# A fourth buffer for the mixed rows, and the norm of two chunks on a pitch of 18 slots

## The chip, the cores and the metric

The kernel runs on one NeuronCore of a Trainium2 chip. The metric is the device time of one execution in microseconds (us); the median of several runs is given. The engines are called TensorE (PE in the profile), VectorE (DVE), ScalarE (ACT), GpSimd (POOL) and SyncE (SP, which only issues DMAs here). SBUF is the on-chip working memory, PSUM the memory into which TensorE accumulates.

## The reference

Attention with a sigmoid in the softmax's place, a two-dimensional Fourier mix of the result, a normalisation and a two-layer network. The batch is 8, with 12 heads, 448 positions, head dimension 64, so d_model is 768; the network's hidden width is 3072.

```python
scores = q @ k.transpose(0, 1, 3, 2) / sqrt(64) - log(448)
x = (sigmoid(scores) @ v)            # then heads side by side: 8 x 448 x 768
u = x + real(fft(fft(x, axis=1), axis=2))
un = (u - mean(u)) / sqrt(var(u) + 1e-6)      # over the last axis
out = u + relu(un @ w_ch1) @ w_ch2
```

## The kernel before

The kernel has three stages. In the **attention stage** a loop runs over 192 slots, two at a time; a slot is a quarter of the positions for one pair of heads, and 24 slots make a batch. For a pair of slots the code issues, in this order: what was put off from the pair before (`sp_next`: writes of u; `act_next`: copies on ScalarE; `dve_next`: sums and adds on VectorE), the score matmuls (L132) and sigmoids (L136), the value matmuls of the pair before (L152) with an eviction on VectorE every four slots (`xT`, L161), some units of the Fourier mix, and the extras.

Each engine takes its instructions strictly in the order in which the code issues them: `pin` chains every instruction to the one before on its engine. So the place of a step in the loop is its place in the queue.

The **mix** of a batch is a list of 36 units (`mix_units`): 24 of `stage_d` (L194), 4 of `stage_s` (L205), 8 of `add_x` (L226). It is taken from while the next batch's attention runs; `mix_some` hands out units by an estimated cost until the budget of 1.14 us for a pair of slots is used up. All units use PSUM tiles of one pool with three buffers (`ps_m`). A unit's evacuation isn't issued with it but put on `act_next` or `dve_next`, so it stands at the start of the next pair. An `add_x` unit transposes three blocks of x into a PSUM tile; VectorE then adds the mix and writes one half of a tile u (L233). A batch has four tiles u, of two halves each; they come from a tag with three buffers. When a tile is full, one or two writes to `u_dram` are put on `sp_next` (L241).

The **extras** hang on slots by `at(t, fn)`. They are, in the order in which they are registered: GpSimd's and VectorE's folds of xT (L175, L178, L181), loads of q, k and v (L106, L107, L113), the casts on GpSimd (L117) and the rests on VectorE (`ql`, `kl`, L122), the scales and the preparation of the weights from slot 170 on (`TP`), and the norm. After the extras of a slot comes the search for the largest weight (`wmax`, L264) and its loads (L259), with three buffers and two tiles of lead.

The **norm** here is that of the first two chunks of 512 rows, needed by the next stage. It goes by halves of 256 rows. `norm_plan` gives the steps of one half chunk with an offset in slots each: 0 the load of 256 rows of u (L332, one buffer); 4 and 5 the statistics of the two blocks of 128 rows (L296, L299); 6 to 10 the reciprocal root, first step three small instructions (L305 to L310), then four steps of four (L315 to L319); 11 and 13 the scaling of a block (L323) and a copy to half precision on ScalarE (L345); 12 and 14 the split on VectorE (L349) and two transposing DMAs on SyncE's queue (L351). The starts before:

```python
for c in range(2):
    for g in range(2):
        for n, fn in norm_plan(c, g, fx):
            at(24 * (4 + 2 * c + g) + LNT + n, fn)      # LNT = 2
```

The four half chunks start at slots 98, 122, 146 and 170. The preparation of one weight tile (`prep_w`) is a chain: load, ScalarE takes the absolute value (L382), VectorE clamps and shifts (L384, L386), merges twice (L390, L392), ScalarE scales (L400), SyncE stores (L401), VectorE takes the rest (L403). Three tiles are made in the last slots; their ScalarE copies stand between the sigmoids.

In the **second stage** (from about 457 us) the first chunk goes through the network while the remaining 45 weight tiles are prepared, two for each of the 24 steps. The **third stage** computes the last five chunks in a fast form. The change touches neither.

Of the kernel before, what the change touches and what calls it, by code (L numbers as in the profile page):

```python
# [9 lines left out]
F32 = mybir.dt.float32  # L10
# [13 lines left out]
DM = 768  # L24
# [12 lines left out]
LNT = 2  # L37
# [21 lines left out]
def spectral_attention_ffn(tc, q, k, v, w1, w2, cd, cs, ident_in, out):  # L59
# [8 lines left out]
    with ExitStack() as top:  # L68
# [19 lines left out]
        if True:  # L88
            c1 = mix.enter_context(tc.tile_pool(name="c1", bufs=1, side="right"))
            fx = mix.enter_context(tc.tile_pool(name="fx", bufs=1, side="right"))  # L90
# [93 lines left out]
            def mix_units(b):  # L184
                xT, xp = xts[b]
                A = fx.tile([HM, 2, 2, 386], F32, tag="A", name="A")
                ps_d, sd, ut = {}, {}, {}

                def stage_d(kp, c, par, p):
                    m = HM - kp  # L190
                    if par == 0 and p == 0:
                        ps_d[c, kp] = ps_m.tile([128, 512], F32, tag="m", name="psd")
                    ps = ps_d[c, kp]
                    nc.tensor.matmul(  # L194
                        ps[:HM, par * 193:par * 193 + 193], xp[:, kp ^ c, c, par, p],
                        cd_sb[:, c, par, p], start=(p == 0), stop=(p == 2))
                    if par == 1 and p == 2:
                        act_next.append(lambda: nc.scalar.activation(
                            A[:, kp, c].rearrange("s (i r) -> s r i", r=2),
                            ps[:HM, 0:386].rearrange("s (r i) -> s r i", r=2), AF.Copy))  # L200

                def stage_s(kp, c):
                    m = HM - kp
                    ps = ps_m.tile([128, 512], F32, tag="m", name="pss")
                    nc.tensor.matmul(  # L205
                        ps[:m, :385], cs_sb[:, kp, c, :m], A[:, kp, c, :385], start=True, stop=True)
                    if c == 1:
                        sd["Q", kp] = Q = fx.tile([128, 385], F32, tag="Q", name="Q", bufs=2)
                        act_next.append(lambda: nc.scalar.activation(Q[:m], ps[:m, :385], AF.Copy))
                    else:  # L210
                        Q = sd["Q", kp]
                        sd[kp] = [fx.tile([128, 385], F32, tag=n, name=n, bufs=2) for n in ("sm", "df")]
                        for o, op in zip(sd[kp], (ALU.add, ALU.subtract)):
                            dve_next.append(lambda o=o, op=op: nc.vector.tensor_tensor(
                                out=o[:m], in0=ps[:m, :385], in1=Q[:m], op=op))

                def add_x(kp, r, hf):

                    lo, hi = (1, HM - 1) if r and not kp else (0, HM - kp)
                    s, d = sd[kp]  # L220
                    if hf == 0:
                        ut[kp, r] = fx.tile([128, DM], F32, tag="u", name="u", bufs=3)
                    u = ut[kp, r]
                    ps = ps_m.tile([128, 512], F32, tag="m", name="psx")
                    for i in range(3):
                        nc.tensor.transpose(  # L226
                            ps[:HM - kp, i * 128:(i + 1) * 128], xT[:, hf * 3 + i, r, kp:HS:2], ident)
                    y = d if hf == r else s
                    m = HM - kp
                    ysl = y[:m, 384:0:-1] if hf else y[:m, 0:384]  # L230

                    def add():
                        nc.vector.tensor_tensor(  # L233
                            out=u[:m, hf * 384:hf * 384 + 384], in0=ps[:m, :384], in1=ysl, op=ALU.add)
                        if hf:
                            base = b * S + (0, 113, 225, 336)[2 * r + kp] - lo

                            cut = lo + (hi - lo) // 16 * 16
                            for i, j in ((lo, cut), (cut, hi)):
                                if i < j:  # L240
                                    sp_next.append(lambda i=i, j=j: nc.sync.dma_start(  # L241
                                        u_dram[base + i:base + j, :], u[i:j, :]))
                    dve_next.append(add)


                res = [(0.33, lambda kp=kp, c=c, par=par, p=p: stage_d(kp, c, par, p))
                       for kp in range(2) for c in (1, 0) for par in range(2) for p in range(3)]
                res += [(0.65, lambda kp=kp, c=c: stage_s(kp, c)) for kp in range(2) for c in (1, 0)]
                res += [(0.31, lambda kp=kp, r=r, hf=hf: add_x(kp, r, hf))
                        for kp in range(2) for r in range(2) for hf in range(2)]  # L250
                return res
# [101 lines left out]
            def norm_plan(c, g, pool):  # L353

                res = [(0, lambda: norm(c, 2 * g, 0, pool))]
                for j in range(2):
                    i = 2 * g + j
                    res += [(LEAD + j, lambda i=i: norm(c, i, 1, pool)),
                            (7 + LEAD + 2 * j, lambda i=i: norm(c, i, 7, pool)),
                            (8 + LEAD + 2 * j, lambda i=i: norm(c, i, 8, pool))]  # L360
                res += [(LEAD + n, lambda n=n: norm(c, 2 * g, n, pool)) for n in range(2, 7)]
                return sorted(res, key=lambda x: x[0])
# [101 lines left out]
            def at(t, fn):  # L464
                extra.setdefault(t, []).append(fn)
# [25 lines left out]
            for c in range(2):  # L491
                for g in range(2):
                    for n, fn in norm_plan(c, g, fx):
                        at(24 * (4 + 2 * c + g) + LNT + n, fn)


            for t in range(0, TQ + LAG + 4, 2):
# [22 lines left out]
        with ExitStack() as fast, ExitStack() as st, ExitStack() as early:  # L520
# [72 lines left out]
            while units or act_next or dve_next or sp_next:  # L593
# [4 lines left out]
                n = step % MIX_STEP  # L598
# [360 lines left out]
```

## Time and profile before

| | us |
|---|---|
| median of 3 runs | 1811.45 |
| the runs | 1807.61, 1811.45, 1819.85 |
| the profiled execution | 1808.63 |
| its span, first to last instruction | 1806.8 |

| engine | busy us | share of the span |
|---|---|---|
| PE | 1670.1 | 92% |
| DVE | 1297.8 | 72% |
| ACT | 603.1 | 33% |
| POOL | 193.6 | 11% |

The shares are means over stages with different limits. Times in the profile are us from the span's start. "x3" behind an instruction counts how many like it were merged, and the text in square brackets is the engine's idle time just before the instruction with the one that ended it. PEclk is the clock that TensorE was granted, as a share of full speed (2.4 GHz; the other level is 1.2).

### The profile page before, as it was taken

What the parts mean: (1) busy time and instruction counts of PE and PEld (TensorE: products, weight loads), DVE (VectorE), ACT (ScalarE), POOL (GpSimd) and SP (SyncE); (2) the same over time, 40 slices, a digit from 0 to 9 for tenths busy, and PEclk for the clock granted to TensorE, in tenths of its full rate; (3) what the DMA queues carried; (4) which work ended last, traced back from release to release, by engine and by line L of the source; (5) the groups of instructions that cost most, each with busy time, mean ns of one, the idle gap of its engine ahead of it and who ended that gap; (6) DMA issues with size and microseconds to landing.
All of it is one profiled execution on the core that took longest, in us unless ns stands there. A gap on an engine that the chain in (4) does not pass through costs nothing. (4 is left out here: it accounts for less than half of the span.)

```text
span 1806.8 us, 27683 instructions
## 1 busy us (share of the span) xinstructions
PE 1670.1 (92%) x10996; PEld 1069.6 (59%) x10996; DVE 1297.8 (72%) x2481; ACT 603.1 (33%) x767; POOL 193.6 (11%) x220
## 2 busy tenths in 40 slices
PE   8999999987777778999879999999999999999997
PEld 4555545543533334555447777677777767776774
DVE  4445576656777776567656888788868887887667
ACT  5444444434333332133224332333133323232221
POOL 4534344334000000000000000000000000000000
PEclk9999999998999999999989999999999999999999
DMA  7666676654666665588887563756476546556551
GB/s 243 214 207 220 222 229 219 207 167 117 217 211 211 211 212 195 182 280 309 294 303 266 227 245 145 280 202 231 152 284 224 217 178 254 216 205 249 215 223 62
DMA packets 109139, 394.95 MB, mean 219 GB/s; under 512 B 23521, under 2 KB 49362, under 8 KB 93522
## 3 DMA queue, kind: packets, MB, share of 16 engines
q1 hardware_dynamic: 109010, 393.19, 61.5%
q8 instruction: 86, 1.41, 0.3%
q14 instruction: 43, 0.35, 0.1%
HBM read 316.08 MB, written 73.92 MB: 216 GB/s over the span
## 5 line engine op out<-in xcount | busy, mean ns | idle before, releaser
L771 PE MATMUL psf<-ut,ws 128*128 128x256 f16 x3780 | 425.4, 274 | 21.4 <-DMA ws<-w_dram 11.7
L822 PE MATMUL pso<-ws,H 128*128 128x384 f16 x2520 | 423.9, 326 | 4.5 <-DVE X L777 1.8
L771 PEld LDWEIGHTS <-ws 128*128 128x128 f16 x3780 | 370.8, 98 | 74.2 <-DMA ws<-w_dram 14.8
L822 PEld LDWEIGHTS <-H 128*128 128x128 f16 x2520 | 246.3, 98 | 160.8 <-issue 5.4
L136 ACT ACTIVATE a<-sc 112x900 f32<-112x900 f32 x192 | 166.8, 918 | 157.0 <-PE sc L132 156.9
L831 DVE TENSOR_TENSOR acc<-pso,acc 128x384 f32<-128x384 f32 x350 | 183.6, 550 | 18.8 <-PE pso L822 18.8
L796 ACT ACTIVATE F<-F 128x1024 f32<-128x1024 f32 x60 | 63.5, 1058 | 357.1 <-DVE F L777 357.1
L557 PE MATMUL po<-w2h,hh 128*128 128x512 f16 (+1 forms) x384 | 131.8, 343 | 52.0 <-ACT hh L545 51.3
L152 PE MATMUL av<-a,vr 112*64 112x450 f32 x768 | 171.1, 568 | 3.8 <-DVE xT L161 3.8
L777 DVE TENSOR_TENSOR H<-F,H 128x1024 f16<-128x1024 f32 x120 | 129.5, 1087 | 48.1 <-ACT H L806 48.1
L538 PE MATMUL psh<-ut,w1h 128*128 128x512 f16 x504 | 151.2, 382 | 3.0 <-DVE hl L546 3.0
L557 PEld LDWEIGHTS <-hh 128*128 128x128 f16 x768 | 76.6, 102 | 108.6 <-ACT hh L545 61.1
L777 DVE TENSOR_TENSOR F<-X,psf 128x256 f32<-128x256 f32 x240 | 96.8, 419 | 51.8 <-PE psf L771 48.0
L557 PE MATMUL po<-w2h,hl 128*128 128x512 f16 (+1 forms) x384 | 130.8, 341 | 1.9
L806 ACT ACTIVATE H<-F 128x1792 f16<-128x1792 f32 x60 | 101.8, 1697 | 88.7 <-DVE F L777 88.7
L557 PE MATMUL po<-w2l,hh 128*128 128x512 f16 (+1 forms) x384 | 131.2, 342 | 0.0
L161 DVE TENSOR_SCALAR xT<-av 128x450 f32<-128x450 f32 x48 | 30.1, 626 | 136.2 <-PE av L152 136.2
L777 DVE TENSOR_TENSOR F<-F 128x256 f32<-128x256 f32 x240 | 91.2, 422 | 24.5 <-ACT F L796 20.5
L132 PE MATMUL sc<-qh,kh 64*112 64x450 f32 x384 | 82.2, 424 | 18.0 <-ACT a L136 13.4
L546 DVE SCALAR_TENSOR_TENSOR hl<-psh,hh 128x512 f16<-128x512 f32 x48 | 33.1, 690 | 90.5 <-ACT hh L545 90.5
L152 PEld LDWEIGHTS av<-a,vr 112*64 112x64 f32 x768 | 47.7, 139 | 82.7 <-issue 67.8
L538 PE MATMUL psh<-ut,w1l 128*128 128x512 f16 x252 | 96.1, 382 | 0.0
(89 smaller groups left out, 1954.9 us busy)
## 6 DMA issues: line engine op xcount, KB each, us to landing
ws<-w_dram SPq DMA_DIRECT2D x120, 1344.0 KB, 8.8
wr<-w_in SPq DMA_DIRECT2D x96, 768.0 KB, 4.9
t_dram<-wt SPq DMA_DIRECT2D x48, 384.0 KB, 2.3
cb<-t_dram SPq DMA_DIRECT2D x24, 768.0 KB, 5.3
qr<-q_in SPq DMA_DIRECT2D x48, 225.0 KB, 3.7
kr<-k_in SPq DMA_DIRECT2D x48, 224.0 KB, 3.4
vr<-v_in SPq DMA_DIRECT2D x24, 448.0 KB
w_dram<-ch SPq DMA_DIRECT2D x24, 384.0 KB, 5.8
```

Of the source, the lines that this page charges most:

```text
L132: nc.tensor.matmul(ps[:CP, j, :SQ], split[g, 1, kn][h, c * CP:(c + 1) * CP], split[g, 0, qn][h], start=(n == 0), stop=(n == 2))
L136: nc.scalar.activation(a, ps[:CP, :, :SQ], AF.Sigmoid, bias=-math.log(S), scale=1.0 / math.sqrt(D))
L152: nc.tensor.matmul(ps[j * D:(j + 1) * D, :SQ], vr[:, c, h * D:(h + 1) * D], a[:, j], start=(c == 0), stop=(c == 3))
L538: nc.tensor.matmul(hs[c, f], l[f][:, m], r[:, m], start=(m == n == 0), stop=(m == NCC - 1 and n == 2))
L546: nc.vector.scalar_tensor_tensor(out=hl, in0=ps, scalar=0.0, in1=hh, op0=ALU.max, op1=ALU.subtract)
L557: nc.tensor.matmul(po[n][:, at:at + hi - lo], l[:, cols], r[f][:, lo:hi], start=(f == 0 and m == 0 and at == 0), stop=(f == NFC - 1 and m ...
L771: nc.tensor.matmul(ps[:, :TH], w[:, x, a, m * 128:(m + 1) * 128], ut[y][:, b, m], start=(m == n == 0), stop=(m == n == 2))
L777: nc.vector.tensor_tensor(out=o, in0=x, in1=y, op=op)
L796: nc.scalar.activation(F[:, 0:4], F[:, 0:4], AF.Relu)
L806: nc.scalar.activation(hts[P][:, 0], F[:, 1:8], AF.Copy)
L822: nc.tensor.matmul(ps[:, :384], H[:, x, a, tp * 128:(tp + 1) * 128], w[:, y, b], start=(j == n == 0), stop=(j == 1 and n == 2))
L831: later(0, lambda: nc.vector.tensor_tensor(out=to, in0=ps[:, :384], in1=to, op=ALU.add))
```

## The change

The tag of the u tiles gets a fourth buffer. The half chunks of the norm start every 18 slots from 98 on: at 98, 116, 134 and 152. The steps and their offsets stay as they are.

```diff
@@ -219,7 +219,7 @@
                     s, d = sd[kp]
                     if hf == 0:
-                        ut[kp, r] = fx.tile([128, DM], F32, tag="u", name="u", bufs=3)
+                        ut[kp, r] = fx.tile([128, DM], F32, tag="u", name="u", bufs=4)
                     u = ut[kp, r]
@@ -491,7 +491,7 @@
             for c in range(2):
                 for g in range(2):
                     for n, fn in norm_plan(c, g, fx):
-                        at(24 * (4 + 2 * c + g) + LNT + n, fn)
+                        at(96 + 18 * (2 * c + g) + LNT + n, fn)
```

## Rows read from the trace of the kernel before

**Rows 1.** Windows: start:end, length, busy us (instructions) per engine, PEclk, DMA share, GB/s
```profile
225.00:270.00 45.00, 41.66 (x247) 22.45 (x245) 32.54 (x57) 20.48 (x27) 20.27 (x23) 0.98 0.73 224
...
540.00:585.00 45.00, 35.44 (x168) 16.84 (x168) 34.16 (x45) 15.80 (x21) 0.00 (x0) 0.92 0.62 210
```
**Rows 2.** Timeline, TensorE, transposes of x: start, us, engine, line, tile, [idle before]
```profile
266.41 0.59 PE L226 MATMUL psx<-ident,xT 128*112 128x128 f32 x3 [2.74 <-DVE u L233]
...
322.44 0.88 PE L226 MATMUL psx<-ident,xT 128*112 128x128 f32 x3 [2.10 <-DVE u L233]
...
370.73 1.25 PE L226 MATMUL psx<-ident,xT 128*113 128x128 f32 x9
...
378.10 0.59 PE L226 MATMUL psx<-ident,xT 128*112 128x128 f32 x3 [1.88 <-DVE u L233]
```
**Rows 3.** Windows of the score matmuls (L132) alone: busy us (instructions) PE, PEld
```profile
0.00:262.42 262.42, 94.36 (x732) 60.80 (x732) 0.99 0.68 220
```
**Rows 4.** Timeline, VectorE, from 262 to 267 us
```profile
262.54 0.63 DVE L161 TENSOR_SCALAR xT<-av 128x450 f32<-128x450 f32 x1 [2.25 <-PE av L152]
...
265.81 1.00 DVE L233 TENSOR_TENSOR u<-psx,df 113x384 f32<-113x384 f32 x2
```
**Rows 5.** Timeline, TensorE, score matmuls after 385 us that had to wait
```profile
411.75 0.72 PE L132 MATMUL sc<-qh,kh 64*112 64x450 f32 x2 [3.40 <-ACT a L136]
...
426.52 0.46 PE L132 MATMUL sc<-qh,kh 64*112 64x450 f32 x2 [2.92 <-ACT a L136]
...
441.97 0.71 PE L132 MATMUL sc<-qh,kh 64*112 64x450 f32 x2 [6.48 <-ACT a L136]
```
**Rows 6.** Timeline, ScalarE, three copies
```profile
367.11 0.49 ACT L209 ACTIVATE Q<-pss 112x385 f32<-112x385 f32 x1 [1.31 <-PE pss L205]
...
409.86 0.94 ACT L400 ACTIVATE w1p<-wt,wsc 128x768 f16<-128x768 f32 x1 [7.68 <-DVE wt L392]
...
424.36 0.82 ACT L345 ACTIVATE hl<-un 128x768 f16<-128x768 f32 x1
```
**Rows 7.** Timeline, VectorE, steps of the norm
```profile
278.73 1.01 DVE L296 BATCH_NORM_STATS2 stt<-un 128x6 f32<-128x384 f32 x2
279.77 0.21 DVE L299 BATCH_NORM_AGGREGATE mv<-stt 128x2 f32<-128x12 f32 x1
...
419.19 0.15 DVE L315 TENSOR_TENSOR mv<-mv 128x2 f32<-128x2 f32 x1
...
419.77 0.16 DVE L319 TENSOR_TENSOR mv<-mv 128x2 f32<-128x2 f32 x1
...
423.40 0.67 DVE L323 TENSOR_SCALAR un<-un,mv 128x768 f32<-128x768 f32 x1
425.21 0.96 DVE L349 TENSOR_TENSOR hl<-un,hl 128x768 f16<-128x768 f32 x1 [1.14 <-ACT hl L345]
...
431.42 1.82 DVE L349 TENSOR_TENSOR hl<-un,hl 128x768 f16<-128x768 f32 x1
```
**Rows 8.** Timeline, VectorE, pairs 164 and 166
```profile
366.84 1.44 DVE L122 TENSOR_TENSOR ql<-qr,qh 128x450 fp32r<-128x450 f32 x1
...
368.73 0.55 DVE L214 TENSOR_TENSOR sm<-pss,Q 112x385 f32<-112x385 f32 x1
```
**Rows 9.** Timeline, SyncE's queue, two transposing DMAs
```profile
352.55 2.56 SPq L351 DMA_TRANSPOSE ut<-hl  x2
```
**Rows 10.** Windows around four gaps of TensorE, columns as in rows 1
```profile
262.42:272.16 9.74, 7.00 (x37) 3.59 (x36) 6.36 (x10) 1.80 (x2) 4.85 (x5) 0.82 0.91 310
...
374.98:382.21 7.23, 5.35 (x37) 3.28 (x35) 4.99 (x9) 1.73 (x2) 1.29 (x1) 1.00 0.85 297
...
411.70:419.29 7.59, 7.54 (x28) 4.16 (x28) 4.09 (x15) 3.65 (x5) 0.00 (x0) 0.57 0.70 230
...
426.50:431.50 5.00, 4.98 (x28) 2.69 (x28) 2.84 (x6) 3.83 (x5) 0.41 (x1) 1.00 1.10 216
```
**Rows 11.** Tile u: its writes' time to landing
```profile
DMA to landing us min/median/max: 2.7/4.1/7.5
```

## The prediction

> **What bounds the kernel now.** I read the windows by stage first. In the stretch from 225 to 270 us TensorE is busy for 41.66 of 45 us and VectorE for 32.54; from 540 to 585 us TensorE has 35.44 and VectorE 34.16 [rows 1]. So the attention is set by TensorE, and the weight stage behind it by a loop in which VectorE is hardly ever free for more than the round trip to ScalarE. Both stages lie one behind the other in every engine's fixed order, so a microsecond by which the attention ends earlier or later moves the end of the kernel by about that much. The rest (two plain chunks, five fast ones) isn't touched.
>
> The second view is TensorE in order of time, read for the gaps. Before 385 us it shows next to none, apart from one in each batch: 2.74 us at 266.41, 2.10 at 322.44, 1.88 at 378.10 [rows 2]. Each stands before the fourth group of transposes of one pair of slots. Up to 262.42 us 732 score matmuls have run, 6 for each slot, so 122 slots: that pair is slots 120 and 121 [rows 3], and the later two are 144/145 and 168/169. The cause is the code: the pacing puts four add_x units into the pair, the PSUM pool has three buffers, and the add that frees the first of the three is issued at the start of the next pair. On VectorE everything of this pair's extras stands ahead of it. In the gap at 266.41 VectorE runs from the eviction at 262.54 (it waits for TensorE) without a pause to the adds at 265.81 [rows 4]. The gap is thus as long as the list of extras, and **any VectorE step put into slots 96, 120, 144 or 168, or the slot after, is paid in full**.
>
> After 385 us there is another pattern: TensorE waits for ScalarE's sigmoid 3.40 us (411.75), 2.92 (426.52) and 6.48 (441.97) [rows 5]. ScalarE's sigmoids stand in its queue behind the copies that scale the prepared weights, and those wait for VectorE's chain, as the copy at 409.86 does for 7.68 us [rows 6]. The last half chunk's norm runs in the same stretch, some of its steps inside that chain.
>
> **The change part by part.** No instruction of the norm is added or removed. Only starts move: half chunk 0 stays at slot 98, the others go from 122, 146, 170 to 116, 134, 152. Within one: load at +0, statistics at +4 and +5, reciprocal root in five steps at +6 to +10, scale at +11 and +13, split and transposes at +12 and +14. So the last step is in slot 166 and not 184, and weight preparation starts at 170.
>
> *What leaves slots 174 to 184.* The chain in pair 176 loses the root's first step, some 0.5 us (three small ones of about 0.16). That in pair 180 loses a root step, 0.66 us from 419.19 to the end of the fourth small instruction [rows 7], and ScalarE's copy of 0.82 us at 424.36, which stands between the scaled weight and the sigmoids [rows 6]. That in pair 184 loses the split at 431.42, 1.82 us [rows 7]. The other norm steps lie where VectorE waits anyway: nothing. Sum 3.8 us earlier. Bounds: 2.9 if the split counts only with the 0.96 us that it takes at 425.21 [rows 7], and 5.5 if two other steps of the chain come free of GpSimd's folds and save the same difference of 0.86 us each. What is late next is the rest of the same chain, so the gap at 441.97 shrinks and doesn't go.
>
> *What arrives in slots 116 to 166.*
> - Pair 120/121 gets both statistics of the second half chunk: twice 1.01 us and 0.21 us [rows 7], 2.4 us. They stand ahead of the adds, so the gap of 2.74 us becomes some 5.2. Before, nothing of the norm was in a pair with four units.
> - Pair 144/145 gets the third one's last root step, 0.66, and its first scale, 0.67 us [rows 7]: 1.3 us at least. A fold of GpSimd waits for the same eviction and runs beside them; the split beside folds took 0.86 longer (1.82 against 0.96 [rows 7]). Between 1.3 and 2.2 I take 1.8.
> - Pair 140/141 gets two root steps, some 1.2 us, ahead of the two sums (seen a batch later, from 368.73, 0.55 each, partly overlapped: to 369.7). The third transpose group, which needs their buffer, starts two thirds into the 1.25 us at 370.73, at 371.56 [rows 2, 8]. Slack 1.8: nothing; up to 0.7 with GpSimd in the way.
> - Pair 164/165: here the order on ScalarE matters. The copy of the second tile is in its queue ahead of the Q copy that now runs at 367.11 [rows 6]. That copy will wait for VectorE: the two rests begin at 366.84 and end at 368.73, 1.89 us [rows 8]; with a split of 0.96 ahead and the scale of 0.67 behind they end at 370.4; copy 0.82, Q 0.49, two sums 1.0 end at 372.7. The third transpose group was due at 371.56: 1.1 us late. Bounds 0 (the scale runs early) and 2 (the split takes 1.82).
> - Pair 128/129: again a copy ahead of sigmoids, but no transpose's buffer hangs on it. Nothing; at most the copy's own 0.82.
> - SyncE's queue: three loads and twelve transposes move. A couple of transposes holds it for 2.56 us at 352.55 [rows 9]; behind it stand loads of the weights, two tiles ahead, and of q and k, issued five slots, over 10 us (122 slots took 262 us [rows 3]), ahead of their cast. Nothing; if that cover were gone, a cast and then the scores would be late by part of 2.56 us.
> - Clock. The pair around the 2.74 us gap has 0.82 of full clock over 9.74 us, that around the 1.88 us gap 1.00 over 7.23 us [rows 10]: of 2.51 us difference 0.86 is the gap and 1.65 the clock, which spends part of the pair at 1.2 GHz. The pair after the 3.40 us gap has 0.57 over 7.59 us, so 3.3 lost [rows 10]. Two longer gaps cost 0 to 1.6 more each; I take 0.8, so 1.6.
>
> Sum of arrivals: 2.4 + 1.8 + 1.1 + 1.6 = 6.9 us; bounds 3.7 (2.4 + 1.3) and 11.5 (2.4 + 2.2 + 0.7 + 2 + 0.8 + 3.2, rounded up). The three old places give nothing back, since TensorE had no gap there.
>
> A rule bears on the second term. The split took 1.82 us beside GpSimd's folds and 0.96 alone [rows 7]. The Trainium skill (SBUF — State Buffer, "Who interferes with whom") says that a VectorE instruction with two SBUF inputs and a GpSimd instruction that reads SBUF exclude each other for a whole instruction. By it pair 144/145 would cost the full 2.2 rather than 1.8, and the statistics, with one input, would keep their 1.01 us; the trace agrees with the direction.
>
> *The fourth buffer.* A batch has four u tiles. With three buffers the fourth tile's first add waits for the first tile's write to land, 2.7 to 7.5 us, median 4.1 [rows 11], and that write is issued about a pair earlier. In the trace no add of u waits for it: at 265.81 VectorE goes straight on [rows 4]. So nothing today. With the new times slot 166's transposes stand in SyncE's queue ahead of batch 5's first write, and the buffer covers that; without it 0 to 3 us once. Its 3 KB a partition move later tiles but put no instruction elsewhere. I take nothing.
>
> **Sum.** 6.9 less 3.8 is 3.1 us later. The profiled execution took 1808.63 us (span 1806.8, 1.8 around it), so 1811.7; that execution is 2.8 below the median of the runs shown, 1811.45. I forecast 1812: no difference that can be told.
>
> **The rivals.**
> 1. The relief wins. If the arrivals cost only their lower bound of 3.7 us, the weights' stretch gives its upper 5.5 and the gap at 411.75 gets short enough to spare the 3.3 us of clock behind it [rows 10], the sum is 5.1 us earlier: 1803.5. For it: all three gaps after 385 us end on that chain [rows 5, 6]. Against it: the chain's larger part is weight steps that stay.
> 2. It gets slower, by the clock. If pairs 120, 144 and 166 each fall to 1.2 GHz as the pair at 411.70 did, they lose 3.3 us each; the first lost 1.65 already and I count the same for the second, so 6.6 come on top of gaps longer by 5.3, less 3.8: 8.1 later, 1817; with the gaps at their upper bounds (8.1) 1820. It decides if the longer gaps leave the pair behind them at 0.57, as the gap of 3.40 us did [rows 5, 10]. For it: the gap of pair 120 should pass that. Against: after 2.92 us at 426.52 the clock stayed at 1.00 [rows 5, 10].
> 3. The change does nothing that shows: VectorE gets to the moved steps earlier, in its waits for TensorE, and the chain after 385 us is set by GpSimd's folds. 1808.6. For it: VectorE has 12 of 45 us free [rows 1]. Against it: its order is fixed, and the free time lies ahead of the eviction, the new steps behind.
>
> **How the numbers follow.** Chances: forecast (1 to 7 us later) 0.45, the first rival 0.22, the second 0.13, the third 0.15, something I don't see 0.05. A measurement of this kernel tells about 1%, 18 us, from no change (the three runs lie 12 us apart). The range takes in all three rivals: 1803 to 1820. Faster by over 1% needs 18 us out of a stretch where the half chunk's norm has some 8.8 on VectorE (2.4 + 0.5 + 4 x 0.66 + 2 x 0.67 + 2 x 0.96 [rows 7]): 0.02. Slower by over 1% needs the upper bounds and something besides: 0.04.
>
> **What would show it.** TensorE's gap in pair 120/121 near 5 us, ending on the add of u, with statistics ahead of it on VectorE; the gap in 144/145 at 3.4 to 4.4; the three gaps on sigmoids still there, the last near 4.7 instead of 6.48; the end of the last attention matmuls within some 5 us of now. I'm wrong if VectorE's extras in pair 120 end before TensorE's third group, if the gaps after slot 170 go altogether, or if a wait on a u write or a weight load shows up.

## The result

| | before | changed |
|---|---|---|
| median of 17 runs each, us | 1814.03 | 1819.49 |
| lowest to highest, us | 1807.47 to 1819.85 | 1814.65 to 1823.55 |
| the profiled execution, us | 1808.63 | 1819.30 |
| its span, us | 1806.8 | 1817.2 |

The ratio is 1.0028, with an interval from 1.0016 to 1.0039: 5.1 us later, between 2.9 and 7.1. That is inside the 1% that was forecast as "no difference", on the side that was forecast, and 2 us more than the sum of 3.1. With 17 runs each it can be told from none; the forecast had said that it couldn't. The two profiled executions lie 10.7 us apart, twice as far as the medians. That of before was 5.4 us below its own median, and 3.1 us of the 10.7 come up behind the attention, which the change doesn't touch; so the difference of those two traces may not be taken whole for the change.

The pages of the two kernels, the one before first, say that the work is the same: each engine has as many instructions, and the busy times differ by little.

```profile
PE 1670.1 (92%) x10996; PEld 1069.6 (59%) x10996; DVE 1297.8 (72%) x2481; ACT 603.1 (33%) x767; POOL 193.6 (11%) x220
...
PE 1675.9 (92%) x10996; PEld 1072.1 (59%) x10996; DVE 1296.7 (71%) x2481; ACT 602.7 (33%) x767; POOL 196.7 (11%) x220
```

Where the time went is seen in TensorE's timeline: start, duration, and in brackets the idle time just before. These are its waits of the changed kernel from 256 us to the end of the attention. They answer to [rows 2, 5].

```profile
269.12 0.84 PE L226 MATMUL psx<-ident,xT 128*112 128x128 f32 x3 [4.21 <-DVE u L233]
...
292.57 0.46 PE L132 MATMUL sc<-qh,kh 64*112 64x450 f32 x2 [0.35 <-ACT a L136]
...
319.98 0.59 PE L226 MATMUL psx<-ident,xT 128*113 128x128 f32 x3 [1.15 <-DVE df L214]
...
328.84 0.91 PE L226 MATMUL psx<-ident,xT 128*112 128x128 f32 x3 [4.02 <-DVE u L233]
...
377.18 0.46 PE L132 MATMUL sc<-qh,kh 64*112 64x450 f32 x2 [2.16 <-ACT a L136]
...
389.64 0.59 PE L226 MATMUL psx<-ident,xT 128*112 128x128 f32 x3 [1.88 <-DVE u L233]
...
401.73 2.62 PE L152 MATMUL av<-a,vr 112*64 112x450 f32 x8 [3.43 <-DVE xT L161]
...
408.39 2.76 PE L194 MATMUL psd<-cd_sb,xp 128*113 128x193 f32 x10 [2.47 <-DVE xp L181]
...
422.79 0.63 PE L132 MATMUL sc<-qh,kh 64*112 64x450 f32 x2 [2.12 <-ACT a L136]
...
434.70 0.46 PE L132 MATMUL sc<-qh,kh 64*112 64x450 f32 x2 [1.48 <-ACT a L136]
...
448.50 0.72 PE L132 MATMUL sc<-qh,kh 64*112 64x450 f32 x2 [4.83 <-ACT a L136]
```

The gaps of 2.74 and 2.10 us have become 4.21 and 4.02, on the same release. The third, 1.88, has no norm step in its pair and is the same. Three gaps are new, 0.35, 1.15 and 2.16. The three on sigmoids shrank from 3.40, 2.92 and 6.48 to 2.12, 1.48 and 4.83. Those at 401.73 and 408.39 aren't new either: the kernel before has 3.82 and 1.68 us there, which the prediction's list of the gaps after 385 us leaves out.

```profile
390.60 3.05 PE L152 MATMUL av<-a,vr 112*64 112x450 f32 x8 [3.82 <-DVE xT L161]
...
396.50 1.89 PE L194 MATMUL psd<-cd_sb,xp 128*113 128x193 f32 x10 [1.68 <-DVE xp L181]
```

A second reading makes a sum of it: the start of each pair's scores in the two traces, subtracted. The changed kernel is 1.24 us later at slot 116, before the first moved step; that is scatter. From there to slot 174 it loses 10.3 us, and the places are sharp:

| slots | later by, us | what stands there |
|---|---|---|
| 120 to 124 | 1.3 | the gap of 4.21 in the place of 2.74 |
| 130 to 134 | 0.5 | the gap of 0.35 |
| 142 to 144 | 1.4 | the gap of 1.15 |
| 144 to 148 | 2.8 | 4.02 in the place of 2.10, and clock |
| 164 to 166 | 2.2 | the gap of 2.16 |
| 166 to 168 | 2.0 | clock, 1.7 of it by the window below |

From slot 174 to the first matmul of the next stage 4.2 us come back (456.17 before, 463.49 after). That difference is 6.6 against a second execution of the old order (experiment 1), so it is known to some 2 us. 10.3 less 4.2 to 6.6 is 3.7 to 6.1, and the 5.1 of the ratio lies within.

The clock is read from windows, columns as in [rows 1]. The first two run from the transposes ahead of the gaps of 4.21 and 4.02 us to the end of the pair behind, the third is pair 166 alone.

```profile
263.66:274.73 11.07, 6.86 (x38) 4.12 (x37) 10.49 (x23) 1.84 (x2) 3.78 (x5) 0.85 0.91 300
323.58:335.33 11.75, 7.73 (x37) 4.35 (x35) 10.54 (x18) 3.53 (x4) 5.22 (x5) 0.71 0.54 108
377.18:383.45 6.27, 6.27 (x30) 2.79 (x30) 4.98 (x9) 3.60 (x5) 2.88 (x3) 0.73 0.46 89
```

The first lost 0.15 of 11.07 us, 1.7; before it was 0.18 of 9.74 [rows 10], 1.75. So a gap longer by half cost no more clock there. The second lost 3.4, the third 1.7 with TensorE busy from end to end: the clock was at 1.2 GHz for a part of it, after the gap of 2.16.

### The profile page after: what moved, and what is told of

It is laid out like the page before. It is cut to its first block, busy times and chain, and to the rows that moved or that the text cites. A ratio compares the mean times of both kernels' runs of the same rounds, so it can differ in the third digit from the quotient of the medians.

```text
span 1817.2 us, 27670 instructions
## 1 busy us (share of the span) xinstructions
PE 1675.9 (92%) x10996; PEld 1072.1 (59%) x10996; DVE 1296.7 (71%) x2481; ACT 602.7 (33%) x767; POOL 196.7 (11%) x220
## 3 DMA queue, kind: packets, MB, share of 16 engines
q8 instruction: 86, 1.41, 0.3%
## 5 line engine op out<-in xcount | busy, mean ns | idle before, releaser
L132 PE MATMUL sc<-qh,kh 64*112 64x450 f32 x384 | 83.1, 428 | 16.7 <-ACT a L136 11.5
```

The source lines that it names most:

```text
L132: nc.tensor.matmul(ps[:CP, j, :SQ], split[g, 1, kn][h, c * CP:(c + 1) * CP], split[g, 0, qn][h], start=(n == 0), stop=(n == 2))
```

## The experiments

Each ratio is against the kernel before on the same chip, and diffs are against the kernel before unless said. In the expectations the letters and names of theories are those of the run: the first mostly is the prediction's reason, that a step costs what it adds to VectorE's list ahead of a wait of TensorE; the other is the rival.

**1. The fourth buffer alone.**
```diff
-   ut[kp, r] = fx.tile([128, DM], F32, tag="u", name="u", bufs=3)
+   ut[kp, r] = fx.tile([128, DM], F32, tag="u", name="u", bufs=4)
```


> The fourth buffer of u alone, the norm's starts as before. Theory A (the starts alone make the change slower: gaps of TensorE in pairs 120, 142, 144 and 162, some 10 us, less a relief of 4 to 5 us after slot 170): no difference, ratio 0.998 to 1.002. Theory B (the slower time comes with the fourth buffer, which moves later tiles in memory): ratio near 1.003, the whole of the change.


1815.36 against 1814.94 us, ratio 0.9998 (0.9981 to 1.0014). By itself the buffer does nothing that can be told from none (to some 0.2%), and neither does the shift of later tiles.

**2. The starts alone**, three buffers.
```diff
-   at(24 * (4 + 2 * c + g) + LNT + n, fn)
+   at(96 + 18 * (2 * c + g) + LNT + n, fn)
```


> The starts every 18 slots with three buffers of u. Theory A: ratio 1.002 to 1.004 as the change, or up to 3 us more, because batch 5's fourth tile would wait for a write that lands 2.7 to 7.5 us after it is issued at about 386 us, some 4.3 us before the add. Theory B: ratio near 1.000.


1818.38 us, 1.0022 (1.0005 to 1.0039). The waits are those of the changed kernel to a hundredth or two (4.21, 0.34, 1.14, 4.02, 2.16). The loss belongs to the starts.

**3. The same pitch of 24 slots, one batch earlier.** Every step stays at its place within a batch, where it cost nothing, and still leaves the last slots.
```diff
-   at(24 * (4 + 2 * c + g) + LNT + n, fn)
+   at(24 * (3 + 2 * c + g) + LNT + n, fn)
```


> Three buffers, and every half chunk of the norm 24 slots earlier than before: starts 74, 98, 122 and 146. So the norm is done by slot 160, ahead of the weights' preparation as in the change, but each step keeps its place within a batch. Theory A: the relief after slot 170 without the new gaps; no gap of TensorE above 2.8 us in pairs 120 and 144; 4 to 5 us faster, ratio 0.9970 to 0.9985. Theory C (there is no relief to be had, the difference after slot 170 is of another origin): ratio 1.000.


1806.35 us, 0.9953 (0.9933 to 0.9974). The gaps ahead of the fourth transposes are 2.74, 2.10 and 1.88 as before, no new one appears, and 8.5 us are gained. So the relief is to be had without any arrivals, and it is larger than I had said: behind slot 174 8.1 us come back, not 3.8. Of the surplus 2.0 us, between slots 174 and 178, lie at a place that the prediction doesn't have: there GpSimd reduces the weights' maxima over the partitions (L272), and the folds behind it wait. This is that row of GpSimd's timeline here:

```profile
391.19 0.37 POOL L272 PARTITION_ALL_REDUCE ws<-wm  x1 [7.34 <-issue]
```

Its input (L270) begins at 386.65, 4.5 us earlier. In the changed kernel the same distance is 7.2 us, in the one before 7.6, in experiment 1 8.1. The profile gives "issue" as the cause, so nothing that it shows.

Another 2.9 us are the clock, which the first rival of the prediction had priced and the forecast had not. In the kernel before, the pair behind the gap of 3.40 us ran at 0.57 of full clock, 3.3 us lost [rows 10]. Here the gap is 2.11 us, the same pair keeps its clock, and takes 2.9 us less. The windows of that pair, here and then in the changed kernel, where the gap is 2.12 us and 1.7 us are lost all the same:

```profile
415.26:419.93 4.67, 4.67 (x28) 2.67 (x28) 2.13 (x4) 3.47 (x5) 1.63 (x1) 1.00 0.99 333
...
422.79:428.91 6.12, 6.12 (x29) 3.72 (x30) 2.13 (x4) 3.52 (x5) 1.64 (x1) 0.72 0.86 284
```

**4. The adds ahead of the extras**, in the pairs whose first slot is a multiple of 24, with the starts of before and four buffers. The sums and adds that a pair has put off are issued behind its mix units and ahead of its extras, and no longer at the start of the next pair.
```diff
-   mix_some(2 * UNIT_US)
+   mix_some(2 * UNIT_US); flush(dve_next if t % 24 == 0 else [])
```


> Starts as before, four buffers of u, and in the pair with four add_x units (every 24th slot) the adds are issued right after the units, ahead of the extras. Theory A (the gap is as long as the extras ahead of the add): the gaps of 1.88 to 2.74 us before the fourth group of transposes shrink to under 0.5 us in every batch; 7 gaps, 14.2 us in all, and some 1.6 us of clock behind three of them: 10 to 17 us faster, ratio 0.990 to 0.995. Rival (TensorE is held there by something else, or the later rests and folds hold the next score matmuls): gaps move to the scores, ratio 0.998 or above.


1793.94 us, 0.9888 (0.9867 to 0.991): 20 us faster, more than the 10 to 17 that I had expected. VectorE's timeline in pair 120 shows the add right behind the eviction, and the rests behind it:

```profile
255.04 0.63 DVE L161 TENSOR_SCALAR xT<-av 128x450 f32<-128x450 f32 x1 [2.25 <-PE av L152]
255.58 1.01 DVE L233 TENSOR_TENSOR u<-psx,df 113x384 f32<-113x384 f32 x2
...
257.44 0.62 DVE L122 TENSOR_TENSOR ql<-qr,qh 128x450 fp32r<-128x450 f32 x1
```

The six gaps ahead of the fourth transposes up to 385 us, 13.4 us together in the kernel before, are gone, and the gaps after slot 170 aren't touched (3.40, 3.25 and 6.50). Between slots 48 and 170 18 us are won by the starts of the pairs. What goes beyond 13.4 is the clock that the gaps cost: between these slots the trace of before has it at 1.2 GHz behind three of the six gaps, 5.1 us lost in all, and the trace of this run nowhere. The wait that the prediction built on is real, and its list of extras is its length.

**5. The same edit with the new starts** (the changed kernel and the line of experiment 4).


> The changed kernel (starts every 18 slots, four buffers), and in every 24th slot the adds of u right after the units, ahead of the extras. Theory A: the gaps of 4.21 and 4.02 us in pairs 120 and 144 go, and with them the loss that the change brought there; the gaps of 1.15 us in pair 142 and 2.16 us in pair 164 stay. Against the kernel before: the 21 us that the same edit gave there, plus or minus 2, ratio 0.986 to 0.990. Rival (the moved steps cost in VectorE's time wherever they stand): still some 5 us behind the same edit on the kernel before, ratio 0.991 or above.


1801.01 us, 0.9922 (0.9899 to 0.9945). If the moved steps cost only by that wait, this would be as fast as experiment 4 or faster. It isn't, and the rival's range is the one that came: 1.0028 times 0.9888 is 0.9916, so the two edits simply multiply. Pair by pair this kernel loses 11.0 us to experiment 4 between slots 116 and 168, where the changed kernel lost 10.3 to the one before. TensorE's timeline shows other waits in the place of the old:

```profile
268.70 1.73 PE L152 MATMUL av<-a,vr 112*64 112x450 f32 x8 [1.88 <-DVE xT L161]
...
320.67 0.46 PE L132 MATMUL sc<-qh,kh 64*112 64x450 f32 x2 [2.16 <-ACT a L136]
...
363.15 0.46 PE L132 MATMUL sc<-qh,kh 64*112 64x450 f32 x2 [2.16 <-ACT a L136]
```

The steps now make VectorE late for its next eviction, or, through a copy, ScalarE late for the sigmoids.

**6. The last half chunk four slots earlier** in the changed kernel, so that it ends further from slot 170.
```diff
-   at(96 + 18 * (2 * c + g) + LNT + n, fn)
+   at((96, 114, 132, 146)[2 * c + g] + LNT + n, fn)
```


> The changed kernel with the last half chunk's norm starting at slot 148 rather than 152, the other three as in the change. Theory A: the gap of 2.16 us in pair 164 (the sigmoids behind a copy that waits for VectorE) goes, the gaps in 120, 142 and 144 stay but for what slot 148's steps add: 3 to 5 us faster than the change, ratio against before 0.999 to 1.001. Rival (that gap comes from GpSimd's folds delaying VectorE at that place whatever the norm does): the gap stays, ratio 1.002 to 1.004.


1813.39 us, 0.9996 (0.9981 to 1.0011), by the two ratios 6 us better than the changed kernel. That is theory A's range, but by luck, for the gap didn't go. It moved with the copy, to the scores of pair 164:

```profile
375.92 0.46 PE L132 MATMUL sc<-qh,kh 64*112 64x450 f32 x2 [2.01 <-ACT a L136]
```

From slot 116 to 174 this kernel loses 10.1 us to the one before, no less than the change. What it wins it wins behind slot 174 (8.6 us come back), where the reduction begins 4.9 us after its input.

**7. Experiments 3 and 4 together**, four buffers.


> The two edits that were faster, together: all norm starts 24 slots earlier than before (74, 98, 122, 146), adds of u ahead of the extras in every 24th slot, four buffers. Theory A: they add up, since one acts before slot 170 and the other behind it: 8.5 and 21 us, ratio 0.982 to 0.986. Rival (what one gives the other takes, as TensorE gets to the weights' chain earlier): ratio 0.988 or above.


1786.97 us, 0.9842 (0.9819 to 0.9866); 0.9953 times 0.9888 is 0.9842. The two gains add up, as theory A had it.

**8. Only the second half chunk moved**, starts at 98, 116, 146 and 170, three buffers.
```diff
-   at(24 * (4 + 2 * c + g) + LNT + n, fn)
+   at((96, 114, 144, 168)[2 * c + g] + LNT + n, fn)
```


> Starts before, but the second half chunk at 116 rather than 122; three buffers. Theory A: the gap of pair 120 is 4.2 us instead of 2.74 and nothing else moves: 1 to 2 us slower, ratio 1.000 to 1.0015. Rival (most of the change's loss is made here): ratio 1.003.


1816.54 us, 1.0014 (0.9995 to 1.0033). The wait in pair 120 is 4.21 us, the next one 0.35, and the others are as before. By the starts of the pairs it loses 1.8 us between slots 116 and 144. Then 1.5 come back: the gap of 2.10 us is there, but the pair behind it keeps its full clock, where the kernel before has 0.71 from 323.25 to 328.05. So the same gap doesn't always cost the clock.

```profile
326.32:329.93 3.61, 3.61 (x26) 1.87 (x25) 2.85 (x5) 1.73 (x2) 2.03 (x2) 1.00 1.05 391
```

The single execution shows the price of this part; its time alone can't be told from none.

**9. Experiment 4 with three buffers.** Here the adds are issued earlier, and the fourth u tile could have to wait for the first one's write.


> Starts as before and the adds of u ahead of the extras in every 24th slot, but with three buffers of u rather than four. Theory A: now the fourth tile's first add stands one pair closer to the first tile's write, which is issued only in the pair behind it, and VectorE waits for it in every batch: TensorE's gaps come back as waits for a u write, 3 to 8 us a batch, so most of the 21 us is lost or more, ratio 0.996 to 1.02. Rival (the fourth buffer is worth nothing here too): ratio 0.987 to 0.990.


1798.44 us, 0.9908 (0.9887 to 0.9929). VectorE does pause ahead of the fourth tile's add, 0.64 us at 100.18 (with four buffers there is no pause):

```profile
98.99 0.55 DVE L233 TENSOR_TENSOR u<-psx,sm 112x384 f32<-112x384 f32 x1
100.18 0.56 DVE L233 TENSOR_TENSOR u<-psx,sm 112x384 f32<-112x384 f32 x1 [0.64 <-PE sc L132]
```

The row names TensorE, but the first tile's write, issued at 94.83, landed at 99.99, 0.2 us before the add, and fits. But TensorE starts its pairs within 0.15 us of experiment 4 to the end of the attention. So the 3 to 8 us for each batch that I had expected aren't there. The medians are 4.5 us apart with intervals that overlap, and the attention doesn't hold that difference. Whether the buffer is worth anything here stays open.

**10. The copy one slot later**, in the changed kernel: ScalarE's copy of a scaled block is issued a slot after the scaling, behind the next sigmoids, and the split a slot after that.
```diff
+                elif n == 8:
+                    u = uns[c, i]
                     hl = wpre.tile([128, 2, DM], F16, tag="wt", name="hl", bufs=3)
                     nc.scalar.activation(hl[:, 0], u, AF.Copy)
...
-                            (8 + LEAD + 2 * j, lambda i=i: norm(c, i, 8, pool))]
+                            (8 + LEAD + 2 * j, lambda i=i: norm(c, i, 8, pool)),
+                            (9 + LEAD + 2 * j, lambda i=i: norm(c, i, 9, pool))]
```


> The changed kernel with ScalarE's copy of a scaled block issued one slot later, behind the next pair's sigmoids, and the split one slot after it. Theory A: the gap of 2.16 us before the scores of pair 166 and the 0.35 us of pair 132 go, as no sigmoid stands behind a copy that waits for VectorE; the Q copy of pair 166 is early again; 2 to 4 us faster than the change, ratio against before 0.999 to 1.001. Rival (VectorE's lateness there, by GpSimd's folds, holds the sums and with them the PSUM buffers anyway): a gap on the sums instead, ratio 1.002 to 1.004.


1814.97 us, 0.9999 (0.9985 to 1.0012), by the two ratios 5 us better than the changed kernel. The gaps of 0.35 and 2.16 on sigmoids are gone, and two others are there:

```profile
377.50 1.73 PE L152 MATMUL av<-a,vr 112*64 112x450 f32 x8 [1.39 <-DVE xT L161]
...
381.80 0.72 PE L226 MATMUL psx<-ident,xT 128*113 128x128 f32 x3 [1.72 <-DVE df L214]
```

From slot 116 to 174 nothing is won against the changed kernel (1.2 us lost): the rival's gap on the sums, with theory A's ratio. The 3.8 us that it wins lie behind that, as in experiments 3 and 6, and the reduction begins 5.4 us after its input. The copy was only the path by which VectorE's lateness reached TensorE first.

**11. All starts of the change six slots earlier** (92, 110, 128, 146), four buffers. The steps fall on other pairs, and the prediction's rule says which gaps follow.
```diff
-   at(24 * (4 + 2 * c + g) + LNT + n, fn)
+   at(90 + 18 * (2 * c + g) + LNT + n, fn)
```


> The pitch of 18 slots kept, all starts six slots earlier: 92, 110, 128, 146, four buffers. Theory A, by place: statistics in pair 96 (its gap 1.88 becomes some 3.3 us), root step and scale in pair 120 (2.74 becomes 4 to 4.7), a copy ahead of sigmoids in pair 138 (a gap of about 2 us before the scores of pair 140), nothing in 144; the last half chunk lies where it costs nothing and the relief behind slot 170 is the full 8 us that the run with all starts 24 slots earlier showed: ratio 0.998 to 1.0015. Rival (any pitch of 18 costs what the change costs): ratio 1.002 to 1.004.


1816.18 us, 1.0003 (0.9987 to 1.0018). TensorE's timeline has the gaps where the rule puts them:

```profile
212.72 0.59 PE L226 MATMUL psx<-ident,xT 128*112 128x128 f32 x3 [3.35 <-DVE u L233]
...
271.50 0.71 PE L226 MATMUL psx<-ident,xT 128*112 128x128 f32 x3 [4.39 <-DVE u L233]
...
318.99 0.46 PE L132 MATMUL sc<-qh,kh 64*112 64x450 f32 x2 [2.20 <-ACT a L136]
...
331.69 0.59 PE L226 MATMUL psx<-ident,xT 128*112 128x128 f32 x3 [2.10 <-DVE u L233]
```

Pair 96 and pair 120 got steps and grew, pair 144 got none and stayed at 2.10. The gap of 2.20 us stands before the scores of pair 142, one pair later than I had said. From slot 96 to 174 this kernel loses 10.2 us to the one before, as much as the changed kernel; it comes out level because 7.9 come back behind that. So half of the rival is right: the moved steps cost about the same here.

**12. The scaled copy of the weights one step later**, on top of experiment 7. For the three tiles that are prepared in the attention, ScalarE's copy (L400) moves from step 3 to step 4 of the chain, where its input is ready.
```diff
-   if n == 3:
+   if n == (4 if i == 0 and f < NPRE else 3):
        nc.scalar.activation(h, t, AF.Copy, scale=sc)
+   if n == 3:
        nc.sync.dma_start(t_dram[i, f // 2][:, 1 - f % 2], t)
-   elif n == 4:
+   if n == 4:
```


> The fastest so far (starts 24 slots earlier, adds ahead of the extras, four buffers), with ScalarE's scaled copy of the three weight tiles of the attention stage issued two slots later, in the step that needs it, so that it no longer stands ahead of the next pair's sigmoids. Theory A (the gaps of 2.11, 1.48 and 4.83 us behind slot 170 are sigmoids behind that copy): they go or shrink below 1 us, 6 to 11 us faster than that kernel, ratio against before 0.978 to 0.981. Rival (the absolute value of the next tile, or GpSimd's folds, hold the same place): ratio 0.983 to 0.986.


1778.03 us, 0.9793 (0.9772 to 0.9814), the fastest kernel of this study: 37 us below the one before, 9 below experiment 7. Of the three gaps on sigmoids one of 0.23 us is left:

```profile
412.85 0.46 PE L132 MATMUL sc<-qh,kh 64*112 64x450 f32 x2 [0.23 <-ACT a L136]
```

## Why the prediction came out as it did

**What held.** The mechanism held: pairs 120 and 144 are paid in the gap ahead of the fourth transposes, on the release by the add of u; the third gap is the same, the three on sigmoids shrink and stay, the last to 4.83 where 4.7 was said. No wait on a write of u or on a weight load appears. Experiments 2, 8 and 11 show the placing. The fourth buffer is nothing by itself, as said (experiment 1). The first and third rival fell: the kernel isn't faster, and the gaps show. Of the second, the clock, a part came true: the pair behind slot 144's gap lost 3.4 us as it says, those behind 120 and 164 half of that. One sign failed: the last attention matmuls end 7.3 us later (461.41 instead of 454.08), not within 5; 1.2 of that is the scatter ahead of slot 116.

The absolute time, 1819.49 us, is 7.5 above the forecast of 1812, at the upper end of the range. 5.4 of that are the base: the sum was put on the profiled execution of 1808.63, and more runs have their median at 1814.03. It was luck that the absolute time still fell into the range, which the rivals had widened. The difference, 5.1 us later, lies in the 1 to 7 of the forecast, and that too is partly luck: too much for pair 120 stands against too little for pairs 140 and 164, and arrivals and relief were both taken too small.

**What was mis-sized.** By the table of slots, the arrivals are 10.3 us where I had 6.9 (bounds 3.7 and 11.5). VectorE's timeline of the changed kernel has the reasons:

```profile
263.78 0.63 DVE L161 TENSOR_SCALAR xT<-av 128x450 f32<-128x450 f32 x1 [2.25 <-PE av L152]
264.32 1.01 DVE L296 BATCH_NORM_STATS2 stt<-un 128x6 f32<-128x384 f32 x2
...
265.99 0.62 DVE L122 TENSOR_TENSOR kl<-kr,kh 128x448 fp32r<-128x448 f32 x1
266.52 1.01 DVE L296 BATCH_NORM_STATS2 stt<-un 128x6 f32<-128x384 f32 x2
...
317.77 1.01 DVE L317 TENSOR_SCALAR mv<-mv 128x2 f32<-128x2 f32 x1
...
318.90 0.56 DVE L214 TENSOR_TENSOR sm<-pss,Q 112x385 f32<-112x385 f32 x1
...
324.43 0.97 DVE L316 TENSOR_TENSOR mv<-mv 128x2 f32<-128x2 f32 x1
...
368.87 0.51 DVE L315 TENSOR_TENSOR mv<-mv 128x2 f32<-128x2 f32 x1
369.42 0.49 DVE L316 TENSOR_TENSOR mv<-mv 128x2 f32<-128x2 f32 x1
369.94 1.01 DVE L317 TENSOR_SCALAR mv<-mv 128x2 f32<-128x2 f32 x1
370.99 0.90 DVE L319 TENSOR_TENSOR mv<-mv 128x2 f32<-128x2 f32 x1
...
374.13 1.31 DVE L323 TENSOR_SCALAR un<-un,mv 128x768 f32<-128x768 f32 x1
```

GpSimd's timeline beside it:

```profile
264.48 0.98 POOL L175 TENSOR_TENSOR eo<-xT 128x450 f32<-128x450 f32 x1 [4.13 <-DVE xT L161]
...
317.70 1.06 POOL L181 TENSOR_TENSOR xp<-fd 128x452 f32<-128x452 f32 x1
...
369.87 1.06 POOL L181 TENSOR_TENSOR xp<-fd 128x452 f32<-128x452 f32 x1
370.89 0.99 POOL L175 TENSOR_TENSOR eo<-xT 128x450 f32<-128x450 f32 x1
371.96 1.92 POOL L178 TENSOR_TENSOR fd<-eo 128x450 f32<-128x450 f32 x2
```

And two rows of VectorE in the kernel before, on record when the prediction was made: the rest `kl` of pair 120 beside a fold, and a small instruction of the root beside another.

```profile
263.62 1.41 DVE L122 TENSOR_TENSOR kl<-kr,kh 128x448 fp32r<-128x448 f32 x1
...
409.75 0.93 DVE L315 TENSOR_TENSOR mv<-mv 128x2 f32<-128x2 f32 x1
```

- *Pair 120/121:* the gap grew by 1.5 instead of 2.4. The statistics took their 2.4 us, but the fold that waits for the same eviction now ran beside the first of them, which kept its 1.01 us. Before, the rest `kl` took 1.41 us there; here it takes 0.62. The Trainium skill (SBUF — State Buffer, "Who interferes with whom") says that a VectorE instruction with at most one SBUF input doesn't contend with GpSimd, outside certain fast modes; the trace agrees, with 1.01 us beside the fold here as without one in [rows 7]. I had used that rule for the length of the statistics and not for what they push out of the fold's way.
- *Pair 144/145:* 1.9 against 1.8 in the gap. The cost above the 1.3 was a small instruction of the root that took 0.97 us beside a fold (324.43).
- *Pair 128/129:* I had nothing, 0.82 at most; 0.5 came, by the copy ahead of the sigmoids.
- *Pair 140/141:* I had nothing, 0.7 at most; 1.4 us came. There a root step that I had at 0.66 us took 2.3, the row at 317.77 in it beside GpSimd's `xp`, and the first sum starts only at 318.90.
- *Pair 164/165:* 1.1 for the second block's copy ahead of Q. The third transposes had no wait. What failed is the step ahead of it: I took root steps at 0.66 us (by [rows 7] 0.74 to the end of the fourth instruction) and overlooked the copy of the *first* block, from slot 163. Two root steps beside GpSimd's folds and casts hold VectorE from 368.87 to the scaling at 374.13, 5.3 us in the place of 1.3. The row at 409.75 had shown it before. The copy waits for that, and the sigmoids behind the copy:

```profile
375.48 0.84 ACT L345 ACTIVATE hl<-un 128x768 f16<-128x768 f32 x1 [6.28 <-DVE un L323]
376.23 1.71 ACT L136 ACTIVATE a<-sc 112x900 f32<-112x900 f32 x2
```

  This ScalarE timeline answers to the gap of 2.16 us on TensorE (2.2 in the table), and the clock behind it costs 1.7 of the 2.0 of the next pair. Together 4.2 in the place of 1.1: the largest miss of the sum.
- *Clock:* 0.8 for pair 120 and 0.8 for pair 144. Measured nothing and about 0.9 (2.8 less the 1.9 of the gap), and 1.7 in pair 166, which had no term. Experiments 3 and 8 show the clock falling or not behind the same gap, so no fixed price for each gap could have been right.
- *Relief:* 3.8 said, 4.2 to 6.6 found. Experiment 3 got 8.1 by the same reading. The three gaps on sigmoids give 1.28, 1.44 and 1.65, 4.4 in all, which is the part that I had. What experiment 3 has on top is 2.0 at the wait for the weights' scale and 2.9 of clock behind the first of the three gaps, less 1.1 behind the last; the changed kernel has 0.8 more instead of 2.0 less at the first place, and 1.4 at the second. The reduction began 6.6 to 8.1 us after its input in five kernels (before, changed, experiments 1, 2 and 8), 4.5 to 5.6 in experiments 3, 6, 10 and 11, and 3.2 to 3.8 in those with the adds first (4, 5, 7, 9, 12). What sets this is not shown: no run changed it by itself.

**The reason was too narrow.** "Any VectorE step put into slots 96, 120, 144 or 168, or the slot after, is paid in full" holds for the place, less what a step takes out of the fold's way (1.5 of 2.4 in pair 120), and isn't the whole. Experiment 5 took that wait away and the moved steps still cost 11 us. In the old places the steps stood where VectorE waited anyway, as experiment 3 shows with the same steps at the same places of another batch; a pitch of 18 slots moves some of them to places where VectorE has no slack, whatever is next in its order. The three old places gave nothing back, as I had said, and that is why even spacing lost.

**What stays open:** the wait ahead of the partition reduction; when a gap costs the clock; the 4.5 us between the medians of experiments 4 and 9; and why the profiled executions differ by 1 to 5 us ahead of the first moved step.

## What to carry to other kernels

Read the slack of each slot before a periodic piece of work gets a new period: one that fits its place in the batch stays free when moved by a whole batch, and was paid for when moved by 6, 12 or 18 slots here. Look at an in-order engine for work that is put off behind what isn't urgent: here the adds behind the extras and a copy that waits ahead of the sigmoids were worth 1.1% and 0.5%, as much as the best of the new starts or more. When one wait is taken away, price the next one in the same queue before calling the steps free.

## What the hardware showed unexpectedly

A VectorE instruction on 128x2 values takes 0.15 to 0.17 us alone. In the attention of the changed kernel 22 of the root's 76 began while an instruction of GpSimd was running, and every one of them ended 0.00 to 0.03 us after that one: after some 0.5 us beside a cast, after up to 1.01 beside a fold of 0.98 to 1.06. So a chain of eight that is 1.3 us by rows grew to 5.3, as it met GpSimd's instructions one after the other. The statistics beside a fold lost nothing (1.01 us). And the partition reduction of 128x2 values, 0.37 us long, began between 3.2 and 8.1 us after its input began, with no row that says for what it waited.
